# Grouped attention beside a Mish layer, one decode step: a quarter of the last wo's rows loaded early in four 8-row transfers

## The chip, the cores and the metric

The kernel runs on one core of one Trainium2 chip. Times are device microseconds of one execution of the whole program. TensorE is called PE, its weight loads PEld, VectorE DVE, ScalarE ACT, GpSimd POOL and SyncE SP, as the profile does.

## The reference

One decode step for 8 sequences, width 512: the normalised input goes through a grouped-query attention over a cache of 8192 keys (32 query heads, 8 key-value heads of 128) and, beside it, through a dense layer with Mish; both results are added to the input. Everything is float32.

```
xn = layernorm(x)
q  = xn @ wq                          # 8 x 32 heads x 128
o  = softmax(q . k / sqrt(128)) @ v   # each kv head serves 4 query heads, 8192 keys
A  = o @ wo                           # 4096 x 512
h  = xn @ w1 + b1                     # 512 x 1792
B  = (h * tanh(softplus(h))) @ w2     # 1792 x 512
out = x + A + B
```

The key and value caches are 256 MiB each, so the kernel is above all one long load.

## The kernel before

The work is cut into 16 packs: a pack `p` is two of the 8 sequences (`b` = 0, 1) for two of the 8 kv heads, and 4 packs make one head pair `i` (0 to 3). For each `(p, b)` one transfer of 8 MiB brings the keys and one the values, each as 128 partition rows of 64 KiB. `scores` (L348) multiplies the keys with the queries, `rows` (L362), `maximum` (L375), `exponents` (L395), `fold` and `weights` make the softmax weights, `values` (L454) multiplies them with v, `gather` (L468) and `merge` (L484) pick and scale the result. `queries` (L308) makes the queries of a head pair from a block of wq, `outputs` (L530) multiplies a finished head pair with its 2 MiB block of wo.

All big loads go through one list, written out at the start in the order in which they are to be moved (`plan`, L114, and the loops L161 to L181). `pump` (L103) issues them on SP's queue as their places come free. There are three places in SBUF: "a" (64 KiB a partition) for v, "b" (80 KiB a partition) for the keys, which lie in it alternately at its start and 16 KiB further on, and "w" (16 KiB a partition) for wq and wo. A transfer over 128 partitions is cut by partition rows over the 16 DMA engines.

The end of that list is what the change touches. v of the last pack's first sequence goes to "b", v of its second to "a" in two parts (3/4 and 1/4 of the columns). Then follow w2 in four parts (2, 2, 2 and 1 sevenths, W2_PARTS, L177) to "b" and the last block of wo to "w" in two halves of its columns, one half (128 rows of 8 KiB) after the second part of w2 and one after the third.

The end of the computation is written out from L695 on. `values` on the two last v; `down` (L623) multiplies the four parts of w2 as they land; `merge` and `turn` (L507) bring the last head pair's attention output into the layout that wo needs: four matmuls into PSUM, then one copy for each 32 partitions j (L526 on ACT for odd j, L528 on DVE for even j) into `oW`, 128 partitions x 4 x 2 x 8. `last_outputs` (L556) multiplies half of oW's columns with each half of wo and adds to the same PSUM tile `H` as `down`. `keep_busy` (L636) puts a matmul of no use into the gaps. At the end DVE copies `H` (L720) and SP stores it (L721). The instructions of PE, DVE and POOL are held in the order of the program (L725 to L740).

One matmul of float32 shows in the trace as two passes: `down` of a 2/7 part has 16 matmuls and 32 passes.

Of the kernel before, what the change touches and what calls it, by code (L numbers as in the profile page):

```python
# [14 lines left out]
B = 8  # L15
# [8 lines left out]
G = 4  # L24
# [3 lines left out]
BW = 1024  # L28
# [4 lines left out]
Q = P // G  # L33
# [5 lines left out]
PAIRS = HKV // 2  # L39
# [3 lines left out]
HE = P // 2  # L43
# [7 lines left out]
KR = DH * 2 * NB // P  # L51
# [12 lines left out]

QR = CC
OR = 4
W1R = 2 * CC * P // P
W2R = G * FT // 2 * FP // P
FAR = 1e38
# [3 lines left out]
def kernel(  # L73
# [12 lines left out]
    nc = tc.nc  # L86
# [27 lines left out]
    def plan(what, at, blocks, parts=((0, 1),), lo=0):  # L114

        rows = rows_of(blocks)
        n = rows.shape[1]
        t = place[at][:, lo : lo + n]

        def load(cols):  # L120
            nc.sync.dma_start(t[:, cols], rows[:, cols])  # L121
            return t

        for first, end in parts:
            cols = slice(round(first * n), round(end * n))
            queue.append((what, at, lambda cols=cols: load(cols)))


    sc = const.tile([P, 512], F32, name="sc")
# [21 lines left out]
    def plan_v(p, b, at, parts=((0, 1),)):  # L151
        plan(("v", p, b), at, blocks_of(v, p, b), parts)
# [1 line left out]
    def plan_wq(i):  # L154
        plan(("wq", i), "w", wq[i * CC : (i + 1) * CC])

    def plan_wo(i, parts=((0, 1),)):
        plan(("wo", i), "w", wo[i * 4 : i * 4 + 4], parts)


    plan_wq(0)  # L161
# [5 lines left out]
    for p in range(PACKS):  # L167
        for b in range(PB):
            plan_k(p, b)
            if (p, b) in between:  # L170
                what, i = between[p, b]
                (plan_wq if what == "wq" else plan_wo)(i)
            if p > 0:
                plan_v(p - 1, b, "a")
    plan_v(PACKS - 1, 0, "b")
    plan_v(PACKS - 1, 1, "a", ((0, 3 / 4), (3 / 4, 1)))
    W2_PARTS = ((0, 2), (2, 4), (4, 6), (6, 7))  # L177
    for k, (lo, hi) in enumerate(W2_PARTS):
        plan("w2", "b", w2, ((lo / W2R, hi / W2R),))
        if 0 < k < 3:  # L180
            plan_wo(PAIRS - 1, (((k - 1) / 2, k / 2),))  # L181


    S = psum.tile([P, GK], F32, name="s")
# [22 lines left out]
    far = const.tile([P, KINDS], F32, name="far")  # L207
# [12 lines left out]
    aT = const.tile([P, 2 * W2R, Q], F32, name="aT")  # L220
    xw = aT.rearrange("p j q -> p (j q)")[:, : W1R * 2 * B]
    xw = xw.rearrange("p (r t b) -> p r t b", r=W1R, t=2)

    def setup():
# [66 lines left out]
    def setup_w1(wide):  # L291
        for r in range(W1R):
            nc.tensor.transpose(  # L293
                M[:, 64 + r * B : 64 + (r + 1) * B], wide[:, r * P : (r + 1) * P], ident[:B, :B]
            )
        for t in range(2):
            nc.vector.tensor_scalar(
                xw[:, :, t, :],
                M[:, 64 : 64 + W1R * B].rearrange("p (r b) -> p r b", r=W1R),
                half[:, t : t + 1],  # L300
                None,
                op0=ALU.mult,
            )

        nc.gpsimd.memset(pt, 0.0)
# [191 lines left out]

    def turning():

        tid = work.tile([P, HT * KINDS * P], F32, name="e", bufs=1)[:, : OR * P]  # L500
        tid = tid.rearrange("p (r g i) -> p r g i", r=OR, g=G)
        nc.vector.tensor_copy(
            tid, ident.rearrange("p (i r o) -> p r o i", r=OR, o=1).to_broadcast([P, OR, G, Q])
        )
        return tid

    def turn(i, tid):  # L507


        to = oW[i] = work.tile([P, OR, 2, B], F32, name="oW")  # L510
        o = oT.pop(i).rearrange("p n h b -> p (n h b)")
        cols = 2 * REP * B
        for r in range(OR):
            nc.tensor.matmul(
                M[:, 256 + r * cols : 256 + (r + 1) * cols],
                tid[:, r].rearrange("p g i -> p (g i)"),
                o,
                start=True,
                stop=True,
            )  # L520
        m = M[:, 256 : 256 + OR * cols].rearrange("p (r j q) -> p j r q", r=OR, j=G)
        for j in range(G):
            rows = slice(Q * j, Q * (j + 1))
            dst = to[rows].rearrange("p r h b -> p r (h b)")
            if i == PAIRS - 1 and j % 2:
                nc.scalar.copy(dst, m[rows, j])  # L526
            else:
                nc.vector.tensor_copy(dst, m[rows, j])  # L528

    def outputs(i, w):  # L530

# [21 lines left out]
                stop=False,  # L553
            )

    def last_outputs(lo, hi, w):  # L556

        for r in range(lo, hi):
            for h in range(2):
                for g in range(G):  # L560
                    at = r * BW + h * D + g * P
                    nc.tensor.matmul(
                        H[Q * g : Q * g + B, :P],
                        oW[PAIRS - 1][:, r, h, :],
                        w[:, at : at + P],
                        start=False,
                        stop=False,
                    )
# [67 lines left out]
    def keep_busy(n):  # L636

        for k in range(n):
            nc.tensor.matmul(C[0][:Q, :], ones[:, :Q], acc, start=True, stop=True)
# [19 lines left out]
    for p in range(PACKS):  # L659
        for b in range(PB):  # L660
            k = landed.pop(("k", p, b))

            n = PB * p + b - (p > 0)
# [15 lines left out]
            if (p, b) in between:  # L679
                what, i = between[p, b]  # L680
# [14 lines left out]
    p = PACKS - 1  # L695
# [12 lines left out]
    w2_sb, wo_sb = landed["w2"], landed["wo", PAIRS - 1]  # L708
    down(*W2_PARTS[0], w2_sb)
    merge(p, 1)  # L710
    turn(PAIRS - 1, tid)
    down(*W2_PARTS[1], w2_sb)
    last_outputs(0, OR // 2, wo_sb)
    keep_busy(1)
    down(*W2_PARTS[2], w2_sb)
    keep_busy(1)
    last_outputs(OR // 2, OR, wo_sb)
    down(*W2_PARTS[3], w2_sb)
    res = acc[:, :P]
    nc.vector.tensor_copy(res, H[:, :P])  # L720
# [3 lines left out]
    last = {}  # L724
# [54 lines left out]
```

## Time and profile before

| what | value |
|---|---|
| median of 3 runs | 1311.35 us (1311.3 to 1311.6) |
| the profiled execution, its own time | 1311.78 us |
| its span in the profile | 1310.0 us |
| PE busy (share of the span) | 863.7 us (66%) |
| DVE busy | 384.0 us (29%) |
| ACT busy | 111.7 us (9%) |
| POOL busy | 4.8 us (0%) |
| mean granted PE clock | 0.844 |
| HBM read | 561.01 MB, 428 GB/s over the span |
| time of the DMA engines taken by SP's queue q1 | 99.3% |

The span is what the profile's time axis shows, from 0 to 1310.0; some 1.8 us of the execution lie around it. "Share of 16 engines" for a DMA queue is the time of its packets over 16 times the span. In a timeline row stand the start, the time taken, engine, line, operation, the tile written and the tile read, the shape, how many instructions were merged, and in brackets the idle time ahead of them with what ended it. In the chain of waits stand start, time taken and what; a "DMA" piece reaches from the issue of a transfer to its landing. In a table of windows stand the window, its length, PE's busy time, the granted clock, the DMA share and GB/s.

### The profile page before, as it was taken

Reading aid. Unit: us, or ns where it says so; the run is one execution under the profiler, and the core shown is the slowest. Engines: PE = TensorE matmul, PEld = TensorE weight load, DVE = VectorE, ACT = ScalarE, POOL = GpSimd, SP = SyncE. Lnnn points to the kernel's source line nnn. Section 1 sums busy time; section 2 is a strip of 40 time slices with the busy share of each in tenths; the row PEclk is TensorE's granted clock in tenths of the full one; section 3 lists DMA queues with packets and bytes.
Section 4 is the critical chain, followed back from the end, with each engine's and each line's share of the span. In section 5 each row is a group of like instructions: output and inputs, shape, how many; then the busy total and the mean of one; then the engine's idle time right before and its main releaser. Section 6 shows DMA issues by size and latency. Waiting matters only on the chain.

```text
span 1310.0 us, 10715 instructions
## 1 busy us (share of the span) xinstructions
PE 863.7 (66%) x4776; PEld 281.5 (21%) x4776; DVE 384.0 (29%) x590; ACT 111.7 (9%) x294; POOL 4.8 (0%) x10
## 2 busy tenths in 40 slices
PE   4786556866557765677565686655875666766657
PEld 1221112212112221122111222111221221222113
DVE  7150504205051230521405032052320505114051
ACT  1020101001010100101101010010100101001010
POOL 1000000000000000000000000000000000000000
PEclk9887889878799877898878897788877879878789
DMA  9999999999999999999999999999999999999997
GB/s 404 442 423 441 433 429 430 434 437 429 438 431 431 431 439 427 439 423 441 421 444 423 419 447 431 435 427 437 423 425 434 429 439 423 439 431 435 439 425 331
DMA packets 11591, 561.76 MB, mean 429 GB/s; under 512 B 1293, under 2 KB 1425, under 8 KB 1561
## 3 DMA queue, kind: packets, MB, share of 16 engines
q1 hardware_dynamic: 11520, 561.06, 99.3%
q8 instruction: 37, 0.61, 0.2%
q14 instruction: 10, 0.07, 0.0%
q10 hardware_dynamic: 24, 0.02, 0.0%
HBM read 561.01 MB, written 0.07 MB: 428 GB/s over the span
## 4 chain that ended last, share of the span: by engine, by line
DMA 67%; PE 32%; DVE 1%; issue 0%; SPq 0%; ACT 0%; ACTq 0%
DMA kvb<-in_kT 60%; PE c L353 30%; DMA kva<-in_kT 3%; DMA kvb<-in_w 2%; DMA kvb<-in_v 2%; PE o L581 0%; PE h L312 0%; PE o L460 0%; DMA sc<-in_x 0%; SPq L121 0%; DVE nm L379 0%; PE s L365 0%; DVE qT L340 0%; PE m L293 0%; PE o L575 0%
## 5 line engine op out<-in xcount | busy, mean ns | idle before, releaser
L353 PE MATMUL c<-kvb,qT 128*64 128x512 f32 x1984 | 502.4, 671 | 347.3 <-DMA kvb<-in_kT 345.7
L353 PEld LDWEIGHTS c<-kvb,qT 128*64 128x64 f32 x1984 | 162.0, 155 | 687.6 <-issue 470.4
L460 PE MATMUL o<-kva,pt 128*32 128x512 f32 x1984 | 231.4, 620 | 24.2 <-DMA kva<-in_v 24.2
L379 DVE TENSOR_REDUCE nm<-s 128x1 f32<-128x1024 f32 x16 | 19.6, 1225 | 462.2 <-PE s L365 462.2
L412 DVE STREAM_TRANSPOSE raw<-e 128x2048 f32<-128x2048 f32 x32 | 116.0, 3626 | 14.4 <-ACT e L404 12.7
L360 ACT COPY sc<-c 128x512 f32<-128x512 f32 x32 | 18.8, 586 | 1005.0 <-PE c L353 1005.0
L460 PEld LDWEIGHTS o<-kva,pt 128*32 128x32 f32 x1984 | 65.7, 113 | 179.3 <-issue 136.2
L404 ACT ACTIVATE e<-s,nms 128x512 f32<-128x512 f32 x128 | 86.3, 686 | 126.1 <-DVE nms L393 66.8
L492 DVE TENSOR_TENSOR oT<-m,r 128x16 f32<-128x16 f32 x16 | 2.8, 175 | 229.6 <-PE m L488 229.6
L471 DVE TENSOR_SCALAR os<-o,isel 128x128 f32<-128x128 f32 x32 | 11.1, 348 | 155.4 <-PE o L460 155.4
L430 DVE TENSOR_TENSOR pt<-raw 64x256 f32<-64x256 f32 x128 | 53.6, 418 | 2.0
L365 PE MATMUL s<-sc,csel 64*128 64x512 f32 x128 | 36.1, 641 | 8.4 <-ACT sc L360 8.4
L421 DVE TENSOR_TENSOR raw<-raw 128x1024 f32<-128x1024 f32 x32 | 39.2, 1225 | 1.1
L340 DVE TENSOR_TENSOR qT<-qc,bsel 128x1024 f32<-128x1024 f32 x32 | 37.6, 1218 | 0.0
L473 DVE SCALAR_TENSOR_TENSOR os<-o,isel,os 128x128 f32<-128x128 f32 x96 | 33.7, 351 | 3.4
L404 ACT ACTIVATION_READ_ACCUMULATOR e<-s,nms 128x1 f32 x128 | 26.0, 203 | 0.0
L380 PE MATMUL m<-ident,nm 128*1 128x128 f32 x16 | 4.3, 270 | 21.2 <-DVE nm L379 21.2
L312 PE MATMUL h<-kvw,xnT 128*64 128x512 f32 x64 | 16.2, 654 | 0.0
L488 PEld LDWEIGHTS m<-hsel,os 128*128 128x128 f32 x64 | 9.5, 188 | 29.6 <-issue 23.5
L488 PE MATMUL m<-hsel,os 128*128 128x8 f32 x64 | 12.4, 266 | 4.8 <-DVE os L473 3.3
L353 PE MATMUL c<-kva,qT 128*64 128x512 f32 x64 | 14.0, 593 | 1.6 <-DMA kva<-in_kT 1.6
L323 DVE TENSOR_SCALAR e<-h 128x512 f32<-128x512 f32 x16 | 9.9, 684 | 15.9 <-PE h L312 15.9
(100 smaller groups left out, 171.4 us busy)
## 6 DMA issues: line engine op xcount, KB each, us to landing
kvw<-in_wq SPq DMA_DIRECT2D x4, 2048.0 KB, 29.7
kvw<-in_wo SPq DMA_DIRECT2D x3, 2048.0 KB, 30.7
kva<-in_v SPq DMA_DIRECT2D x1, 6144.0 KB, 27.2
kva<-in_w SPq DMA_DIRECT2D x1, 3584.0 KB, 15.8
kvb<-in_w SPq DMA_DIRECT2D x3, 1024.0 KB, 20.6
kva<-in_v SPq DMA_DIRECT2D x1, 2048.0 KB
kvw<-in_wo SPq DMA_DIRECT2D x2, 1024.0 KB, 24.6
kvb<-in_w SPq DMA_DIRECT2D x1, 512.0 KB
```

The lines of the kernel that those rows point to most:

```text
L340: nc.vector.tensor_mul(qT[:, b], qc[:, k * PB + b] .rearrange("p r (o h) -> p r o h", o=1) .to_broadcast([P, KR, KN, REP]), bsel.rearrange ...
L353: nc.tensor.matmul(C[b][HE * c : HE * (c + 1), :], t[:, r], k[:, r * BW + c * 512 : r * BW + (c + 1) * 512], start=(r == order[0]), stop=( ...
L360: nc.scalar.copy(sc, C[b])
L365: nc.tensor.matmul(S[:, c * 512 : (c + 1) * 512], csel[HE * c : HE * (c + 1), b].rearrange("p u b h -> p (u b h)"), sc[HE * c : HE * (c + ...
L379: nc.vector.tensor_reduce(nm, S, axis=AX.X, op=ALU.max, negate=True)
L404: nc.scalar.activation(ex[:, :, s, :], S[:, c * 512 : (c + 1) * 512].rearrange("p (t f) -> p t f", t=HT), AF.Exp, bias=NMS[p][:, s : s + 1 ...
L412: nc.vector.transpose(raw.rearrange("p (m t r) -> p t m r", m=TW, t=HT), ex.rearrange("p t s (q m) -> p t m (s q)", m=TW),)
L421: nc.vector.tensor_add(raw[:, :, :n], raw[:, :, :n], raw[:, :, n:])
L430: nc.vector.tensor_add(pt[rows, b, c].rearrange("p m t e h -> p (m t) e h")[:, :, e], raw[rows, :, at : at + REP], raw[rows, :, V8 + at : ...
L460: nc.tensor.matmul(O[b][Q * c : Q * (c + 1), :], pt[:, b, j % 2, j // 2].rearrange("p t e h -> p (t e h)"), vt[:, W4 * DH * j : W4 * DH * ...
L473: nc.vector.scalar_tensor_tensor(os, O[b][:, DH * i : DH * (i + 1)], isel[:, i : i + 1], os, op0=ALU.mult, op1=ALU.add,)
L488: nc.tensor.matmul(M[:, at : at + 2 * REP], OS.pop((p, b)), hsel, start=True, stop=True)
```

## The change

The last block of wo is 128 rows of 16 KiB. It is no longer loaded as two halves of its columns, but by rows:

- Every fourth row (3, 7, 11, ..., 127) comes ahead of the last v, in four transfers of 8 whole rows. The 16 of them below 64 go to their own partitions of "w" ("near"). The 16 from 64 on go 64 partitions lower, to the same partitions 3, 7, ..., 63, but into the last 16 KiB of "b" ("far"), which the last keys used and the first of the two last v does not.
- The other rows come where the halves came, both after the second part of w2: the even rows in one transfer of 64 rows, then rows 1, 5, 9, ... in one of 32.
- POOL sets the upper 64 partitions of "w" and the lower 64 partitions of the far place to zero ahead of the loads, so that rows which are not there multiply as zero.
- `turn` writes the last head pair's output a second time, partitions 64 to 127 copied to partitions 0 to 63 of the tile `sc` (one copy on DVE, one on ACT).
- `last_outputs` now runs twice over all 4 row groups: once with the far rows and that copy (64 partitions deep), once with the near place, one directly behind the other between the second and the third part of w2. The two filler matmuls there are gone.

```
+QS, QH = 4, 3
...
+    OX_AT = KR * BW
+    last_wo = rows_of(wo[(PAIRS - 1) * 4 :])
+
+    def plan_wo_far():
+
+        n = last_wo.shape[1]
+        near = place["w"][:, :n]
+        far = place["b"][:HE, OX_AT : OX_AT + n]
+
+        def load_near():
+            nc.gpsimd.memset(near[HE:], 0.0)
+            for k in range(QH, 8, QS):
+                nc.sync.dma_start(near[k:HE:8], last_wo[k:HE:8])
+            return near
+
+        def load_far():
+            nc.gpsimd.memset(far, 0.0)
+            for k in range(QH, 8, QS):
+                nc.sync.dma_start(far[k:HE:8], last_wo[HE + k :: 8])
+            return far
+
+        queue.append((("wo", PAIRS - 1), "w", load_near))
+        queue.append(("wo far", "behind b", load_far))
+
+    def plan_wo_rest(first, step):
+        n = last_wo.shape[1]
+        t = place["w"][:, :n]
+
+        def load():
+            nc.sync.dma_start(t[first::step], last_wo[first::step])
+            return t
+
+        queue.append((("wo", PAIRS - 1), "w", load))
...
     plan_v(PACKS - 1, 0, "b")
+    plan_wo_far()
     plan_v(PACKS - 1, 1, "a", ((0, 3 / 4), (3 / 4, 1)))
     W2_PARTS = ((0, 2), (2, 4), (4, 6), (6, 7))
     for k, (lo, hi) in enumerate(W2_PARTS):
         plan("w2", "b", w2, ((lo / W2R, hi / W2R),))
-        if 0 < k < 3:
-            plan_wo(PAIRS - 1, (((k - 1) / 2, k / 2),))
+        if k == 1:
+            plan_wo_rest(0, 2)
+            plan_wo_rest(1, 4)
...
+        if last:
+
+            oX = oW["far"]
+            for j in range(G // 2, G):
+                rows = slice(Q * j, Q * (j + 1))
+                dst = oX[Q * j - HE : Q * (j + 1) - HE].rearrange("p r h b -> p r (h b)")
+                if j % 2:
+                    nc.scalar.copy(dst, m[rows, j])
+                else:
+                    nc.vector.tensor_copy(dst, m[rows, j])
...
-    def last_outputs(lo, hi, w):
-
-        for r in range(lo, hi):
+    def last_outputs(o, w):
+
+        for r in range(OR):
             for h in range(2):
                 for g in range(G):
                     at = r * BW + h * D + g * P
                     nc.tensor.matmul(
                         H[Q * g : Q * g + B, :P],
-                        oW[PAIRS - 1][:, r, h, :],
+                        o[:, r, h, :],
...
     merge(p, 1)
+
+    oW["far"] = sc[:HE, : OR * 2 * B].rearrange("p (r h b) -> p r h b", r=OR, h=2)
     turn(PAIRS - 1, tid)
     down(*W2_PARTS[1], w2_sb)
-    last_outputs(0, OR // 2, wo_sb)
-    keep_busy(1)
+    last_outputs(oW["far"], landed["wo far"])
+    last_outputs(oW[PAIRS - 1], wo_sb)
     down(*W2_PARTS[2], w2_sb)
-    keep_busy(1)
-    last_outputs(OR // 2, OR, wo_sb)
     down(*W2_PARTS[3], w2_sb)
```

More of the change, by code (lines that the diff above doesn't have):

```diff
@@ L155, in plan_wq, with plan_wo @@
         plan(("wq", i), "w", wq[i * CC : (i + 1) * CC])
-    def plan_wo(i, parts=((0, 1),)):
-        plan(("wo", i), "w", wo[i * 4 : i * 4 + 4], parts)
+    def plan_wo(i):
+        plan(("wo", i), "w", wo[i * 4 : i * 4 + 4])
+    OX_AT = KR * BW
[23 more added lines that the diff above has]
+        queue.append((("wo", PAIRS - 1), "w", load))
     plan_wq(0)
@@ L507, in turn @@
     def turn(i, tid):
+        last = i == PAIRS - 1
         to = oW[i] = work.tile([P, OR, 2, B], F32, name="oW")
@@ L524, in turn @@
             dst = to[rows].rearrange("p r h b -> p r (h b)")
-            if i == PAIRS - 1 and j % 2:
+            if last and j % 2:
                 nc.scalar.copy(dst, m[rows, j])
```

## The prediction

> **What bounds the kernel now.** I read the page's transfer rows first, then the chain of waits, then the end of the span with the DMA view cut into narrow windows.
>
> ```profile
> span 1310.0 us, 10715 instructions
> ...
> DMA  9999999999999999999999999999999999999997
> ...
> DMA packets 11591, 561.76 MB, mean 429 GB/s; under 512 B 1293, under 2 KB 1425, under 8 KB 1561
> ...
> q1 hardware_dynamic: 11520, 561.06, 99.3%
> q8 instruction: 37, 0.61, 0.2%
> ...
> q10 hardware_dynamic: 24, 0.02, 0.0%
> ```
>
> The 16 DMA engines are busy in every slice but the last, and one queue, q1 (SP's), fills 99.3% of their time. A kernel like this ends when the slowest of 16 engines has moved its share. At 429 GB/s an engine moves 26.8 GB/s, so a 16 KiB row costs one engine 16384 / 26.8e3 = **0.61 us**. That is the unit of this forecast.
>
> The chain of waits at its end, in order of time (start, us, what):
>
> ```profile
> 1247.64 25.68 DMA kvb<-in_v
> ...
> 1278.57 1.21 SPq L121
> ...
> 1279.82 26.57 DMA kvb<-in_w
> 1306.39 0.04 issue
> 1306.43 0.67 PE h L628 x16
> ```
>
> The last transfer, the last seventh of w2, lands at 1306.39. Behind it stand only 16 matmul passes, then a copy and the store. An earlier last landing moves the end by as much, until PE is late instead.
>
> Now the stagger of the engines. Three windows over the time in which the first three quarters of the last v land, the first data that the tail works on; then the drain from 1300 to 1306.4 in 40 slices of 0.16 us. Each engine ends its part of a transfer with one packet under 512 B, so that count says how many engines are done.
>
> ```profile
> DMA packets 38, 0.75 MB, mean 343 GB/s; under 512 B 8, under 2 KB 8, under 8 KB 8
> ...
> DMA packets 35, 0.59 MB, mean 421 GB/s; under 512 B 5, under 2 KB 5, under 8 KB 5
> ...
> DMA  9596969898897969564636366503122322100000
> GB/s 666 205 563 256 563 282 512 358 461 358 358 410 307 384 256 384 230 282 179 256 154 256 154 256 205 230 26 128 77 102 102 128 102 102 77 26 26 0 0 0
> ...
> q1 hardware_dynamic: 286, 1.49, 56.4%
> ...
> 1287.91 4.69 PEld L460 LDWEIGHTS o<-kva,pt 128*32 128x32 f32 x48 [0.46 <-DMA kva<-in_v]
> ```
>
> Between 1283.0 and 1285.2 **eight** engines finish, between 1285.2 and 1286.6 five more, and the last three only by 1287.9, where PE, released by that transfer, loads its first weights for it. So eight engines run early, at least 2.7 us ahead of the last. No later transfer mends it, since each gives every engine an equal share. The drain shows the same: from the 28th slice (1304.3) never more than 128 GB/s, five engines' worth. The rest of the work is 56.4% of 6.4 us = 3.61 us of all 16 engines: shared out evenly it would end near 1303.6. **No rebalancing of this tail can win more than 2.8 us.**
>
> Why eight? The page counts 37 instruction fetches on q8, 16 KiB each. Following each data packet to the one that begins where it ends (the packet records, which no view prints), I find the fetches falling in turn on eight engines only, and these are the late ones. This sets chances below, no term.
>
> **The change part by part.** *The short transfers.* An 8-row transfer uses eight engines, one row each: q10 holds the x load (8 rows) and the b1 load (4 rows) and shows 24 packets, 12 rows and 12 completions; a transfer over all 16 would add 16 completions. After the change eight engines get 4 early rows, and the two remaining transfers give each of 16 engines 4 + 2 rows. Before, each engine had the equivalent of 8. So the eight carry 10 rows (+2, **+1.22 us**), the others 6 (−2, **−1.22 us**). I take the eight to be the early ones.
>
> [...] The four engines that I followed from the b1 load all seem to be of the early kind, one with a doubt.
>
> *Late engines.* Last landing 1306.39 − 1.22 = 1305.17; the third part of w2 (1 MiB, 64 KiB on each engine, 2.44 us; the last part, 32 KiB, 1.22 us) lands at 1303.95, the rest of wo at 1301.51. *Early engines.* At least 2.7 us ahead, so done by 1303.7, with 1.22 more by 1304.9: still not last. On the way they are 4 rows (2.44 us) later on the last v and on w2's first half, less than their 2.7 us lead, so PE's starts there stay. Gain on the landing: **1.22 us**.
>
> *SP's queue and POOL.* Two of the short transfers stand behind a memset of 64x4096, and the last v behind them on SP.
>
> ```profile
> 1234.44 16.59 PE L353 MATMUL c<-kvb,qT 128*64 128x512 f32 x64 [10.60 <-DMA kvb<-in_kT]
> ...
> 1247.64 0.33 SPq L121 DMA_DIRECT2D kvb<-in_v  x1
> 1260.69 0.33 SPq L121 DMA_DIRECT2D kva<-in_v  x1
> ...
> 11.09 2.12 DVE L286 COPY csel<-ident 64x64 f32<-64x64 f32 x4
> 11.29 1.84 POOL L305 MEMSET pt<- 128x2048 f32 x1 [1.20 <-PE m L293]
> ...
> 1254.85 0.21 DVE L386 COPY nx<-nr 1x128 f32<-1x128 f32 x1
> ```
>
> The memset may start when the last score matmul has read that place, 1234.44 + 16.59 = 1251.03. The nearest row is 2048 elements in 1.84 us: 4096 should take 3.7 (an estimate; at least 1.84), so it ends about 1254.7. Two issues follow at 0.33 (this row) to 1.21 us each (1278.57 above): SP is free by 1257.1. Before, SP issues the last v only at 1260.69, waiting for PE. Cover 3.6 us: cost **nothing**; it would cost only with a memset over 7 us, and even then up to 1268 or so the queue still holds the transfer issued at 1247.64. The other memset waits for wo's third block, long used. The rest of wo and w2's last two parts wait on SP for the four short transfers; these end behind the last v but one on the early engines, about when that lands as a whole (1247.64 + 25.68 = 1273.3), and SP issues that part of the tail only around 1278.57: nothing again. A memset can hold up DVE: at 11.29 the four small copies beside it took 2.12 us instead of some 0.2 each. The copy nx at 1254.85 comes just behind; if the memset ran 0.5 us longer, so would what follows, and 0.3 of it is covered (below). Value 0, bounds 0 and +0.5.
>
> *PE and the copies.* The timeline of the tail:
>
> ```profile
> 1298.57 1.06 PE L628 MATMUL h<-kvb,aT 128*8 128x128 f32 x32
> 1298.68 0.21 DVE L528 COPY oW<-m 32x64 f32<-32x64 f32 x1 [1.20 <-PE m L514]
> 1298.92 0.20 ACT L526 COPY oW<-m 32x64 f32<-32x64 f32 x1 [33.75 <-DVE oW L528]
> ...
> 1299.42 0.20 ACT L526 COPY oW<-m 32x64 f32<-32x64 f32 x1 [0.29 <-DVE oW L528]
> ...
> 1300.33 1.06 PE L562 MATMUL h<-kvw,oW 128*8 128x128 f32 x32 [0.70 <-DMA kvw<-in_wo]
> 1301.20 1.02 PE L639 MATMUL c<-acc,ones 128*32 128x512 f32 x2
> ...
> 1305.18 1.06 PE L562 MATMUL h<-kvw,oW 128*8 128x128 f32 x32 [0.56 <-DMA kvw<-in_wo]
> 1306.43 0.62 PE L628 MATMUL h<-kvb,aT 128*8 128x128 f32 x16 [0.19 <-DMA kvb<-in_w]
> ```
>
> The copies alternate between DVE and ACT, each waiting for the other, about 0.25 apart; two more end at 1299.42 + 0.20 + 2 x 0.25 = 1300.12. 32 passes take 1.06, 16 take 0.62: 0.0275 a pass plus 0.18 at the end. Added are 64 passes for the far rows (1.76 us); removed are the two filler matmuls of 1.02. Then: far 1300.17 to 1301.93; near (rest of wo landed 1301.51) to 1303.69; third part of w2 at its landing, 1303.99 to 1304.9; last part at 1305.21, ending 1305.21 + 0.62 = 1305.83. Before, 1306.43 + 0.62 = 1307.05. PE waits 0.3 us for each of the last two landings: that is the cover of the added 1.76 us, of the two copies and of a late DVE. Without it, each microsecond there is paid in full.
>
> *The clock without the fillers.* Two pairs of PE windows (us, PE busy, granted clock, DMA):
>
> ```profile
> 1212.50:1215.90 3.40, 0.99 (x10) 1.00 1.16 501
> 1215.90:1219.30 3.40, 3.40 (x20) 0.50 0.93 405
> 1301.25:1304.65 3.40, 2.87 (x44) 1.00 0.63 255
> 1304.65:1308.05 3.40, 1.68 (x48) 1.00 0.08 31
> ```
>
> With 0.99 us of work in 3.4 the clock was halved right after; with 1.68 it still stood at 1.00. In the new tail any such window holds about 1.8 us or more, so I take no loss; half a clock on the last 16 passes and part of those before would be +0.3 to +0.9.
>
> **Sum:** −1.22 + 0. The profiled execution took 1311.78 (1310.0 and 1.8 around it) and should be 1310.56; the median shown is 0.43 lower, 1311.35, so **1310.1 us**. The change is −0.09%, below what a measurement of this kernel tells from no change (0.2%, 2.6 us).
>
> **Rivals.** *The short rows collide (slower side).* All 32 early rows go into partitions 3, 7, 11 ... 59, so two of the eight engines may write into one place at a time. If pairs in step share one engine's rate, 4 rows cost 4.88 us instead of 2.44, and the early engines end up to 2.44 later: 1304.9 + 2.44 = 1307.3 instead of 1306.39, so 1311.35 + 0.95 = **1312.3**. It decides from 0.3 us extra on, where the early become last, and turns into a loss from 1.5. The same bound holds if PE starts late on the last v: its chain then ends with that landing. Against it: at 429 GB/s in all, engines are at full rate in each stage, and pairs out of step by a row would not meet. Chance 0.14, any price between 1310.4 and 1312.3.
>
> [...]
>
> *The eight are the late ones.* Then these carry +1.22: 1311.35 + 1.22 = **1312.6**. The followed packets speak against it: 0.05. *PE becomes the bound* through the copies, the 64 passes, DVE behind the memset or the halved clock: **1310.4 to 1311.0**, 0.07. *Nothing is shifted*, the rows being spread over 16 engines: **1311.3**, 0.02. *A stall of SP or a broken order of landings* over 2.6 us: 0.03. *More than forecast*, at most 2.8 us by the drain: 1308.5, 0.01.
>
> **How the numbers follow.** The forecast, 1310.1, has the remaining 0.68, with its own range 1309.7 to 1310.5. The range 1309.6 to 1311.7 takes in that, PE as bound, the unshifted case and about half of the collisions, 0.84 in all; left out are late eight, hard collisions and the stall. Only the stall and part of its neighbours lie over 2.6 us slower: 0.04. Over 2.6 us faster: 0.01. Within: 0.95.
>
> **What would show it.** Right: the window of the drain holds fuller slices up to 1304.9 and is empty after 1305.2; last landing of in_w near 1305.2; PE's far passes start near 1300.2 with ACT as the releaser; a POOL memset of 64x4096 of about 3.7 us near 1251; SP's last v still near 1260.7; PEclk 1.00 in the tail. Wrong: PE starting on the last v after 1287.9 (collision, or the late eight); eight engines still moving after 1306; L628 waiting for PE rather than for in_w; nx later than 1255; a halved clock after 1301.

## The result, and the profile after

| | before | after |
|---|---|---|
| median | 1311.45 us (1311.30 to 1311.63, 6 runs) | 1316.35 us (1314.69 to 1317.51, 6 runs) |
| profiled execution, its span | 1311.78, 1310.0 | 1314.69, 1312.9 |

The ratio is 1.0037, with a 95% interval of 1.0024 to 1.005: the change makes the kernel slower by about 4.9 us. The forecast was 1310.1, with a range that ended at 1311.7. The profiled execution of after is the fastest of its six, so its trace shows 2.9 us of the loss.

The rows of the page of after that answer to those of before. The work is the same, and so is the share of the one queue. The rate (GB/s) stands lower in one of the 40 slices, the last but one (some 1247 to 1280 us): 383 in place of 425. The last has 330 and had 331. First before's row of rates, then the rows of after.

```profile
GB/s 404 442 423 441 433 429 430 434 437 429 438 431 431 431 439 427 439 423 441 421 444 423 419 447 431 435 427 437 423 425 434 429 439 423 439 431 435 439 425 331
```

```profile
span 1312.9 us, 10849 instructions
...
DMA  9999999999999999999999999999999999999997
GB/s 403 443 432 430 440 428 424 440 430 436 431 436 436 428 432 438 422 444 424 436 431 424 432 436 430 440 424 438 422 436 435 428 434 438 422 446 418 440 383 330
...
q1 hardware_dynamic: 11424, 561.06, 99.3%
```

The DMA engines are as busy in that slice as in the others (9) and move less. Busy is not fast: a packet that takes longer counts as busy for longer. To find the place, three windows of each kernel, first before, then after. The columns are the length of the window, the busy times of PE, PEld, DVE, ACT and POOL with their instructions, the granted PE clock, the DMA share and GB/s.

```profile
1256.00:1266.00 10.00, 6.73 (x62) 1.99 (x54) 7.10 (x9) 5.47 (x16) 0.00 (x0) 1.00 0.99 427
1268.00:1276.00 8.00, 2.54 (x13) 0.69 (x17) 6.29 (x10) 0.00 (x0) 0.00 (x0) 0.50 0.97 418
1278.00:1288.00 10.00, 8.53 (x67) 2.86 (x63) 1.57 (x5) 0.00 (x0) 0.00 (x0) 1.00 0.97 414
```

```profile
1256.00:1266.00 10.00, 6.64 (x54) 1.81 (x46) 8.27 (x11) 3.69 (x12) 0.00 (x0) 0.94 1.05 448
1268.00:1276.00 8.00, 0.40 (x4) 0.23 (x8) 5.09 (x10) 0.00 (x0) 0.00 (x0) 0.50 1.03 285
1278.00:1288.00 10.00, 8.53 (x69) 2.90 (x62) 1.57 (x5) 0.00 (x0) 0.00 (x0) 0.84 0.96 415
```

In the 8 us from 1268 the rate falls from 418 to **285 GB/s** at a DMA share of 1.03, and it stands at 415 again from 1278 on (414 before). That is when the short rows move (1267.6 to 1276.2 in the packet records, which no view prints): they are queued behind the transfer that before's chain shows landing at 1273.3. In those 8 us (418 − 285) x 8 = 1.06 MB stay unmoved, 2.5 us of all 16 engines at 429 GB/s. Half the rate on the eight engines with short rows alone would leave three quarters, some 314 of 418; 285 is lower. That **the other engines are slowed too** is in the packet records as well: the 16 KiB rows took 0.65 to 1.3 us (half of them 0.98 or more) in place of 0.61, and the 64 KiB packets of ordinary rows that begin in this window 3.6 to 4.4 in place of 2.42. Followed from packet to packet, each of the eight engines without short rows has long ones: seven of them 64 KiB packets, the longest of each 3.48 to 3.91 us, the eighth 48 KiB packets of 2.83 and 2.85 in place of 1.82.

What this does further on, first two rows of before, then the timeline of after (`o` is what the last two v are multiplied into; L639 and L689 are the filler matmuls ahead of the last v):

```profile
1273.46 8.97 PE L460 MATMUL o<-kvb,pt 128*32 128x512 f32 x64 [7.98 <-DMA kvb<-in_v]
...
1284.77 3.60 PE L639 MATMUL c<-acc,ones 128*32 128x512 f32 x8
```

```profile
1249.32 3.50 POOL L179 MEMSET kvb<- 64x4096 f32 x1 [149.78 <-PE c L392]
...
1252.85 1.17 SPq L181 DMA_DIRECT2D kvb<-in_wo  x2
1253.07 0.22 DVE L425 COPY nx<-nr 1x128 f32<-1x128 f32 x1
...
1260.60 0.34 SPq L124 DMA_DIRECT2D kva<-in_v  x1
...
1275.61 9.82 PE L499 MATMUL o<-kvb,pt 128*32 128x512 f32 x64 [11.33 <-DMA kvb<-in_v]
...
1287.76 4.86 PE L689 MATMUL c<-acc,ones 128*32 128x512 f32 x7
...
1292.04 0.63 PE L499 MATMUL o<-kva,pt 128*32 128x512 f32 x3
...
1304.60 0.21 ACT L576 COPY sc<-m 32x64 f32<-32x64 f32 x1 [0.28 <-DVE sc L578]
...
1304.90 1.93 PE L612 MATMUL h<-kvb,sc 64*8 64x128 f32 x64 [0.58 <-issue]
1306.76 1.93 PE L612 MATMUL h<-kvw,oW 128*8 128x128 f32 x64
...
1308.51 1.49 PE L678 MATMUL h<-kvb,aT 128*8 128x128 f32 x48
1310.07 0.29 DVE L770 COPY acc<-h 128x128 f32<-128x128 f32 x1 [5.51 <-PE h L678]
```

PE starts on the last v at 1292.04; in the kernel before, it did so at 1287.92. Two things are late there, each by about as much. One is that transfer's landing (KB, us from issue to landing, first before, then after): issued at 1260.7 and 1260.6, it lands at 1287.9 and 1291.7.

```profile
kva<-in_v SPq DMA_DIRECT2D x1, 6144.0 KB, 27.2
```

```profile
kva<-in_v SPq DMA_DIRECT2D x1, 6144.0 KB, 31.1
```

The other is PE itself. The v ahead of it lands at 1275.5 in place of 1273.3, after PE has been idle for 11.33 us in place of 7.98, and from 1276 to 1292 PE was granted a lower clock (first two windows before, then two after; the clock stands ahead of the DMA share):

```profile
1276.00:1284.00 8.00, 6.76 (x58) 2.10 (x50) 1.40 (x5) 0.00 (x0) 0.00 (x0) 0.92 1.01 432
1284.00:1292.00 8.00, 7.78 (x57) 3.55 (x61) 0.17 (x2) 0.00 (x0) 0.00 (x0) 1.00 0.93 393
```

```profile
1276.00:1284.00 8.00, 8.00 (x56) 2.20 (x52) 0.00 (x0) 0.00 (x0) 0.00 (x0) 0.68 0.96 412
1284.00:1292.00 8.00, 6.53 (x34) 1.94 (x27) 1.57 (x5) 0.00 (x0) 0.00 (x0) 0.79 0.95 407
```

The multiplication with that v took 9.82 us in place of 8.97, and the fillers were still running when the last v had landed; before, PE's weight loads sat idle for 0.46 us until that landing. From 1292 on PE's chain runs without a wait for a transfer: the far pass at 1304.90, the near pass at 1306.76, the last two parts of w2 in one run of 48 passes, to 1310.00. Before, the last pass ended at 1307.05: 2.95 us earlier, which is the difference of the spans (2.9). The drain, in the same window as in the prediction, shows that the transfers are late by themselves: where before's slices stood at 0 by 1306.4, the last five here are still at 2 to 6 tenths.

```profile
DMA  9299949793959696989949797979696958352665
...
q1 hardware_dynamic: 320, 2.25, 84.1%
```

### The profile page after: what moved, and what is told of

Its sections match the earlier page's. It is cut to its first block, busy times and chain, and to the rows that moved or that the text cites. A ratio compares the mean times of both kernels' runs of the same rounds, so it can differ in the third digit from the quotient of the medians.

```text
span 1312.9 us, 10849 instructions
## 1 busy us (share of the span) xinstructions
PE 864.9 (66%) x4836; PEld 281.6 (21%) x4836; DVE 385.0 (29%) x591; ACT 111.9 (9%) x295; POOL 11.9 (1%) x12
## 4 chain that ended last, share of the span: by engine, by line
DMA 60%; PE 35%; DVE 4%; issue 1%; ACT 0%; SPq 0%; ACTq 0%; DVEq 0%
DMA kvb<-in_kT 54%; PE c L392 31%; PE o L499 3%; DMA kva<-in_kT 3%; DMA kvb<-in_v 2%; DMA kva<-in_w 1%; DVE raw L451 1%; DVE pt L469 1%; PE o L631 0%; DVE os L512 0%; PE c L689 0%; DVE nm L418 0%; DVE raw L460 0%; PE s L404 0%; PE h L612 0%
## 5 line engine op out<-in xcount | busy, mean ns | idle before, releaser
L392 PE MATMUL c<-kvb,qT 128*64 128x512 f32 x1984 | 495.7, 663 | 350.4 <-DMA kvb<-in_kT 316.7
L499 PE MATMUL o<-kva,pt 128*32 128x512 f32 x1984 | 236.7, 630 | 22.8 <-DMA kva<-in_v 22.8
L499 PE MATMUL o<-kvb,pt 128*32 128x512 f32 x64 | 9.8, 782 | 11.3 <-DMA kvb<-in_v 11.3
```

The costliest lines, as they stand in the source:

```text
L392: nc.tensor.matmul(C[b][HE * c : HE * (c + 1), :], t[:, r], k[:, r * BW + c * 512 : r * BW + (c + 1) * 512], start=(r == order[0]), stop=( ...
L499: nc.tensor.matmul(O[b][Q * c : Q * (c + 1), :], pt[:, b, j % 2, j // 2].rearrange("p t e h -> p (t e h)"), vt[:, W4 * DH * j : W4 * DH * ...
```

## The experiments

Theories at the start. **P**: rows that different engines write into neighbouring partitions collide in SBUF (the prediction's rival). **S**: source rows 128 KiB apart collide where they are read. **E**: a transfer over eight engines alone slows everything. A fourth, **H**, was formed from the runs. Each edit is against the changed kernel unless said; a kernel that ran once has one time and no interval. "The window" is 1268 to 1276 us; the last number of its row, the rate, says whether the dip is there.

**e1_step4.** The same rows, but each 8-row transfer takes every fourth partition in place of every eighth.

```diff
-            for k in range(QH, 8, QS):
-                nc.sync.dma_start(near[k:HE:8], last_wo[k:HE:8])
+            for k in (QH, QH + 32):
+                nc.sync.dma_start(near[k : k + 29 : 4], last_wo[k : k + 29 : 4])
...
-            for k in range(QH, 8, QS):
-                nc.sync.dma_start(far[k:HE:8], last_wo[HE + k :: 8])
+            for k in (QH, QH + 32):
+                nc.sync.dma_start(far[k : k + 29 : 4], last_wo[HE + k : HE + k + 29 : 4])
```

> Same rows early, but each 8-row transfer takes every fourth row of one quarter (3 to 31, 35 to 63, 67 to 95, 99 to 127), written to partitions 4 apart; source rows 64 KiB apart instead of 128. In the changed kernel the DMA engines together fall from 418 GB/s (kernel before) to 285 in the window 1268 to 1276. Theory P (the 8 rows written 8 partitions apart collide in SBUF): back over 400 GB/s in that stretch, time 1310.1 to 1312.6 (the upper end if two of the eight engines are late ones). Theory S (8 source rows 128 KiB apart collide in HBM): at least partly better, 1311 to 1315. Theory E (a transfer over eight engines alone slows all): unchanged, about 285 GB/s and 1315 to 1317.

Measured: 1312.55 (1311.16 to 1314.36, 10 runs) against 1311.51, ratio 1.0008, interval 0.9999 to 1.0018. The window of e1:

```profile
1268.00:1276.00 8.00, 3.01 (x16) 0.89 (x20) 5.95 (x10) 0.00 (x0) 0.00 (x0) 0.52 0.98 424
```

The dip is gone (285 to 424 GB/s), and with it 3.8 of the 4.9 us. E falls: these transfers too have 8 rows, and those of after went over eight engines (packet records, as above). About 1 us of loss is left between the medians, though the interval just takes in none; e7 and e14 look into it.

**e2_src_contig** and **e3_dst_step4.** One alters the source only, the other the destination only. So e2 loads other rows of wo than the computation's, and e3 puts the right ones into wrong partitions; the amounts are the same. First e2's edit, then e3's.

```diff
-                nc.sync.dma_start(near[k:HE:8], last_wo[k:HE:8])
+                nc.sync.dma_start(near[k:HE:8], last_wo[2 * (k - QH) : 2 * (k - QH) + 8])
```

```diff
-                nc.sync.dma_start(near[k:HE:8], last_wo[k:HE:8])
+                nc.sync.dma_start(near[QH + 8 * (k - QH) : QH + 8 * (k - QH) + 29 : 4], last_wo[k:HE:8])
```

The far rows are altered in the same way.

> Written as in the changed kernel, 8 partitions apart, but each transfer reads 8 neighbouring rows of wo (16 KiB apart), so the wrong rows of wo are multiplied. Theory P: about 285 GB/s in the stretch of the short rows, 1314.7 to 1317.5. Theory S: over 400 GB/s, 1310 to 1312.6. Theory E: about 285 GB/s.

> Read as in the changed kernel (source rows 128 KiB apart), but written to partitions 4 apart (3 to 31, 35 to 63), so rows of wo meet the wrong rows of the attention output. Theory P: over 400 GB/s in the stretch, 1310 to 1312.6. Theory S: about 285 GB/s, 1314.7 to 1317.5. Theory E: about 285 GB/s.

Measured: e2 1314.9, e3 1312.1 (one run each). The window of e2, then of e3:

```profile
1268.00:1276.00 8.00, 0.26 (x4) 0.23 (x8) 6.42 (x10) 0.00 (x0) 0.00 (x0) 0.50 1.03 279
```

```profile
1268.00:1276.00 8.00, 2.84 (x16) 0.91 (x20) 5.62 (x10) 0.00 (x0) 0.00 (x0) 0.50 1.03 442
```

The destination decides, the source doesn't: S falls.

**e4_rows16.** Two transfers of 16 rows, by the expectation over all 16 engines, every fourth partition of the lower half.

```diff
+            for k in (QH,):
+                nc.sync.dma_start(near[k:HE:4], last_wo[k:HE:4])
...
+            for k in (QH,):
+                nc.sync.dma_start(far[k:HE:4], last_wo[HE + k :: 4])
```

> The same 32 rows come early, but as two transfers of 16 rows over all 16 engines, one row each, partitions 4 apart; no engine gets more than another. Theory E: over 400 GB/s and the time of the kernel before, 1311.0 to 1311.6. Theory P: two engines a place, as in the changed kernel, so below 400 GB/s for some 5 us, 1312.5 to 1315. Theory S: over 400 GB/s, 1311.0 to 1312.

Measured: 1315.45 (1314.36 to 1317.33, 9 runs), ratio 1.003, interval 1.002 to 1.004; 291 GB/s in the window. The partitions are those of e1; only the cut into transfers differs, and with it, as the expectation takes it, the engines that write them. The dip is back (291 GB/s in place of 424), so it is not the partitions alone; what is left is which engine writes which.

**e5_direct.** As e1, but the upper rows go to their own partitions (67 to 127); no far place, no memset, no second pass.

```diff
+            for k in (QH, QH + 32, QH + 64, QH + 96):
+                nc.sync.dma_start(near[k : k + 29 : 4], last_wo[k : k + 29 : 4])
```

> As the variant with steps of 4, but the rows of the upper half go to their own partitions (67 to 95, 99 to 127), so there is no far place, no memset, no second copy of the output and no second pass of 64. If engines of the upper half write there at their full rate already, theory P (places collide) says that these two transfers slow the machine again: about 300 GB/s for half as long as in the changed kernel (some 4 us), 1312 to 1314. If P holds only between the short rows themselves: over 400 GB/s throughout and, PE having 1.76 us less to do, 1310.0 to 1311.5.

Measured: 1314.94 (1313.22 to 1316.57, 10 runs), ratio 1.0025, interval 1.0015 to 1.0034; 301 GB/s in the window. The detour of the upper rows by the lower half, with its 64 passes, is worth more than it costs: written straight into the upper half, they dip.

**e7_no_far_pass.** As e1, without the 64 passes on the far rows, so that these are missing from the sum. It asks whether e1's last 1 us is PE's.

```diff
-    last_outputs(oW["far"], landed["wo far"])
```

> The variant with steps of 4 without the 64 passes over the far rows, so these rows' part of the result is left out; loads as there. If what is left of its loss (median 1312.55, 1311.16 to 1314.36) is PE becoming the bound: 1310.1 to 1311.3 and a spread under 1.5 us. If it is two late engines among the eight: unchanged, 1312 to 1313 with the same spread.

Measured: 1312.61 (1310.46 to 1313.29, 10 runs), ratio 1.0005, interval 0.9995 to 1.0014. With 1.9 us of PE work less it is no faster than e1, so the rest isn't that pass's. Its profiled execution (1312.76) ends behind the last transfer, which lands at 1307.4, 1.0 us later than before's (1306.39):

```profile
1279.47 27.95 DMA kvb<-in_w
```

**e6_adjacent** and **e8_half.** e6 puts each transfer's 8 rows into 8 neighbouring partitions (again wrong ones for the computation); e8 is e1 for the far rows and the changed kernel for the near ones.

```diff
+                nc.sync.dma_start(near[4 * (k - QH) : 4 * (k - QH) + 8], last_wo[k:HE:8])
...
+                nc.sync.dma_start(far[4 * (k - QH) : 4 * (k - QH) + 8], last_wo[HE + k :: 8])
```

```diff
+            for k in (QH, QH + 32):
+                nc.sync.dma_start(far[k : k + 29 : 4], last_wo[HE + k : HE + k + 29 : 4])
```

> As the changed kernel, but each 8-row transfer writes 8 adjacent partitions (0 to 7 or 16 to 23), so rows of wo meet wrong rows of the output. If a place is 4 neighbouring partitions, four rows meet in each of two places: theory P says worse than the changed kernel, under 250 GB/s while they move and 1317 to 1322. If only a distance of 8 collides: over 400 GB/s, 1311 to 1313.

> Near rows as in the changed kernel (8 apart), far rows 4 apart. Theory P: half the dose, the low rate (about 285 GB/s) for some 4 us instead of 8.5, time 1312.5 to 1315. If any collision sets the whole loss: 1314.7 to 1317.5.

Measured (one run each): e6 1317.57 and 242 GB/s in the window; e8 1315.33 and 293. The window of e6:

```profile
1268.00:1276.00 8.00, 0.00 (x0) 0.00 (x0) 6.28 (x10) 0.00 (x0) 0.00 (x0) 0.50 1.05 242
```

Neighbouring partitions gave the lowest rate of these runs, 242 GB/s. Half the dose dips as deep in this window, and by the packet records below it costs less in all (37 engine-us in place of 53).

**e9_ladder.** A try to tell the eight engines apart: transfers of 1, 2, ... 8 rows, 36 in all, in their own partitions; no far place and no second pass. All 36 are loaded again with the rest, in two transfers of 64 rows.

```diff
+            for n, k in enumerate((0, 1, 2, 3, 32, 33, 34, 35)):
+                nc.sync.dma_start(near[k : k + 4 * n + 1 : 4], last_wo[k : k + 4 * n + 1 : 4])
```

> To tell the engines apart: ahead of the last v eight transfers of 1, 2, ... 8 rows, partitions 4 apart in the lower half, so that the first engine gets eight extra rows, the next seven, and so on (all 36 are loaded again with the rest; one pass of 64 at the end, no far place, no memset). With 36 rows (0.59 MB) more in all the time says little: 1312 to 1316. Rate while the short rows move: over 400 GB/s, as no two of one transfer share a place. If two of the first eight engines are late ones: two of the eight ladders belong to engines that are hit by instruction fetches. If none: no ladder is hit.

Measured: 1317.75 (one run), for a reason of its own. SP's issues in e9:

```profile
1246.35 0.33 SPq L124 DMA_DIRECT2D kvb<-in_v  x1
1246.73 26.69 SPq L173 DMA_DIRECT2D kvw<-in_wo  x8
1273.53 0.85 SPq L124 DMA_DIRECT2D kva<-in_v  x2
```

Eight transfers behind the 8 MiB one keep SP for 26.69 us; the last v is issued at 1273.53 (1260.60 in after), and the engines run dry (8 GB/s from 1272 to 1274). Two and two (1.39 and 1.17 us of SP in after) cost nothing. What SP waited for between the eight (us in total, times, longest):

```profile
SPq L173 <- DMA kvb<-in_v: 18.6, 1, 18.6
...
SPq L173 <- DMA kva<-in_v: 2.6, 1, 2.6
```

So the hold is above all a wait for the 8 MiB transfer's landing. In the trace's records the transfers share eight landing semaphores in turn: the eighth short one takes that of the 8 MiB one and is issued when that has landed, at 1272.7. The question that the ladder was for stayed unanswered; that each of its transfers begins with the same engine, as the expectation takes it, no run shows.

**e10_rows16_low.** Only 16 early rows, 1, 5 ... 29 and 3, 7 ... 31, at their own partitions; the rest as transfers of 64 and 48 rows.

```diff
+            for k in (1, 3):
+                nc.sync.dma_start(near[k : k + 29 : 4], last_wo[k : k + 29 : 4])
...
-            plan_wo_rest(1, 4)
+            plan_wo_rest(33, 2)
```

> 16 early rows instead of 32 (1, 5, ... 29 and 3, 7, ... 31, 4 apart, in their own partitions), the other 112 rows in two transfers over all 16 engines; no far place, no memset, no second pass, PE has the passes of the kernel before. Half the shift: +0.61 us on the eight, -0.61 on the others. If two late engines among the eight set the end: 1311.8 to 1312.3, half the loss of the variant with 32 rows 4 apart (+1.0). If the eight were all early ones: 1310.6 to 1311.0.

Measured: 1318.28 (1317.52 to 1319.75, 4 runs), ratio 1.0054, interval 1.0037 to 1.007: a miss. Three windows of e10:

```profile
1268.00:1276.00 8.00, 2.64 (x16) 0.78 (x20) 6.15 (x10) 0.00 (x0) 0.00 (x0) 0.50 0.99 426
...
1292.00:1300.00 8.00, 6.45 (x82) 2.94 (x70) 1.99 (x7) 0.20 (x1) 0.00 (x0) 1.00 1.07 353
1300.00:1308.00 8.00, 1.28 (x36) 0.92 (x40) 0.03 (x1) 0.21 (x1) 0.00 (x0) 0.56 0.86 214
```

The early rows run clean, and the dip sits in the tail, where the 48-row transfer (33, 35 ... 127: three rows for each engine, if they are shared out evenly) moves. The chain of waits ends behind its landing, at 1307.8:

```profile
1278.01 29.76 DMA kvw<-in_wo
```

Which engine writes which of its rows no record says.

**e11_home.** Two transfers of 16 rows, 3, 11 ... 123 and 7, 15 ... 127, at their own partitions, to control for whole rows that come early. The edit is against e5. I took engine j's ordinary rows to be the eight partitions 8j to 8j+7.

```diff
-            for k in (QH, QH + 32, QH + 64, QH + 96):
-                nc.sync.dma_start(near[k : k + 29 : 4], last_wo[k : k + 29 : 4])
+            for k in (QH, QH + 4):
+                nc.sync.dma_start(near[k::8], last_wo[k::8])
```

> The 32 early rows go by two transfers of 16 rows (3, 11, 19 ... 123 and 7, 15 ... 127), one row on each of the 16 engines, each row into a partition that its engine also writes in the ordinary transfers; no far place, no second pass, no memset. P (rows written by engines of two kinds into one place at a time): no collision, 425 GB/s or more from 1268 to 1276 us, and since no engine carries more than another nothing is shifted: 1311.2 to 1311.8, within 0.05% of the kernel before, and PE starts on the last v near 1288. If it is enough for a collision that whole 16 KiB rows come early (any partition): 270 to 310 GB/s in that window and 1314 to 1316. If e1's loss of 1.0 us comes from the order of the transfers and not from two late engines among the eight: 1312.3 to 1312.8 with a clean window.

Measured: 1315.45 (1314.75 to 1316.49, 7 runs), ratio 1.0028, interval 1.0017 to 1.004; the window of e11:

```profile
1268.00:1276.00 8.00, 0.47 (x4) 0.23 (x8) 5.72 (x10) 0.00 (x0) 0.00 (x0) 0.50 1.00 272
```

P in this form falls. What fits all the runs is **H**, a supposition: no record names the engine that moved a packet or the partition that it went to, so H is judged by the rates alone, its engine numbers stand for the order of the rows, and what makes two writers slow each other in one place no run shows. H supposes that each engine has a home, the partitions that it writes in the ordinary transfers, that row j of an 8- or 16-row transfer goes to engine j, and that a row which an engine writes in another's home meets the ordinary rows that the owner is writing there. The homes are fitted to the rates from 1268 to 1276 us:

- Row j of an 8-row transfer runs clean at partitions 3+4j and 35+4j (e1, 424 GB/s) and at 1+4j (e10, 426), and not at a step of eight (after, 285) or of one (e6, 242). So engine j (0 to 7) gets 1+4j to 3+4j and the same 32 higher. 4j and 32+4j are counted with them, though no run speaks for it: of the early rows only some of e6 and e9 lie there.
- The upper half is not home to these eight (e5, 301), and 16 rows that all go to the lower half dip (e4, 291). So engine 8+j gets the same 64 higher; no run tells one of these eight from another.

In e1, each row is at home. In the changed kernel row j goes to 3+8j or 7+8j: one of eight at home.

**e12_shift.** The test of H against P: as e1, but the near rows land four partitions higher (7, 11 ... 35 and 39, 43 ... 67) and the far ones in 6, 10 ... 34 and 7, 11 ... 35, so that it sums other rows than the computation's; the edit is against e1. No two rows of a transfer share a home, but none is at its own.

```diff
-                nc.sync.dma_start(near[k : k + 29 : 4], last_wo[k : k + 29 : 4])
+                nc.sync.dma_start(near[k + 4 : k + 33 : 4], last_wo[k : k + 29 : 4])
...
-            for k in (QH, QH + 32):
+            for k in (6, 7):
```

> As e1 (8-row transfers, step 4), but the rows go four partitions (far: three or four) higher: 7, 11 ... 35 and 39, 43 ... 67, far 6, 10 ... 34 and 7, 11 ... 35. Wrong rows, and the far pass reads them, so that the output is not the reference's; bytes, engines and passes are those of e1. Within one such transfer no two rows lie in the same group of four partitions or 32 apart, just as in e1; but row number j of each lies where, by the runs so far, engine j+1 writes its ordinary rows, and in e1 where engine j itself does. P (two of the short rows in one place at a time): no collision, 425 GB/s or more from 1268 to 1276 us and 1312.0 to 1312.9. H (each engine has a place of its own, two groups of four partitions 32 apart, and a row written into another engine's place collides with that engine's ordinary rows): 250 to 310 GB/s there and 1314 to 1317. H is what e11 calls for: its 16 rows, row j to partition 3+8j, lie at home for engines 0 and 8 alone.

(What it says of e11 holds, by H, for the first of its two transfers; in the second, engines 7 and 15 are at home.) Measured: 1317.54 (1316.67 to 1320.05, 5 runs), ratio 1.0048, interval 1.0034 to 1.0062; two windows of e12:

```profile
1268.00:1276.00 8.00, 0.00 (x0) 0.00 (x0) 6.92 (x10) 0.00 (x0) 0.00 (x0) 0.50 1.03 285
1276.00:1284.00 8.00, 7.04 (x56) 2.18 (x60) 0.00 (x0) 0.00 (x0) 0.00 (x0) 0.76 0.94 350
```

**H holds and P falls**: four partitions of shift cost 5.0 us (1312.55 to 1317.54), though no two rows of one short transfer share a home.

**e13_home32** and **e14_extra16.** e13 loads the 32 early rows by one transfer over all 128 partitions, two rows for each engine, if they are shared out evenly, and needs no far place. e14 loads 16 rows a second time by two transfers of 8 rows, at home by H, which nothing reads. e13's edit is against e11, e14's against e13.

```diff
-            for k in (QH, QH + 4):
-                nc.sync.dma_start(near[k::8], last_wo[k::8])
+            for k in (QH,):
+                nc.sync.dma_start(near[k::4], last_wo[k::4])
```

```diff
+            for k in (QH, QH + 32):
+                nc.sync.dma_start(far[k : k + 29 : 4], last_wo[k : k + 29 : 4])
```

> The 32 early rows by one transfer (rows 3, 7 ... 127 to partitions 3, 7 ... 127), two rows on each of 16 engines; no far place, no second pass, no memset. H (each engine has a place of its own: two groups of four partitions, 32 apart) with the ordinary rows shared out by that place: each engine gets the two rows of its own place, so no collision, 425 GB/s or more from 1268 to 1276 us, and as no engine carries more than another the time of before: 1311.1 to 1311.8. If rows that come early collide wherever their transfer reaches over all 128 partitions (as e5, e11 could also be read): 270 to 310 GB/s and 1314 to 1316.

> e13 and two transfers of 8 rows more (step 4, to partitions 3 ... 31 and 35 ... 63 of the far place), which load 16 rows a second time and which nothing reads: two rows more on each of the eight engines that carry them, 1.22 us each, none on the others; each row at home by H, so a clean window. If two late engines are among the eight (the reading of e1 and e7): 1.0 to 1.3 us over e13. If all eight are early, as the prediction took it: 0 to 0.3 over e13. If the rows were spread over all 16 engines: 0.6.

Measured: e13 1311.51 (1311.17 to 1313.16, 11 runs) against 1311.57, ratio 0.9998, interval 0.9989 to 1.0007; e14 1312.25 (1311.40 to 1314.14, 11 runs), ratio 1.0005, interval 0.9996 to 1.0014. The window of e13, then of e14:

```profile
1268.00:1276.00 8.00, 2.83 (x16) 0.91 (x20) 6.05 (x10) 0.00 (x0) 0.00 (x0) 0.50 0.95 412
```

```profile
1268.00:1276.00 8.00, 3.23 (x16) 0.90 (x20) 5.44 (x10) 0.00 (x0) 0.00 (x0) 0.50 1.02 440
```

Early rows over all 128 partitions can run clean and take the time of before. That each lies at home supposes that this transfer, too, is shared out by home; with that, it settles what e5 and e11 left open. The medians of e13 and e14 are 0.74 us apart, between the 0 to 0.3 for early engines and the 1.0 to 1.3 for late ones, nearest to the 0.6 for rows spread over 16 engines, and the runs overlap. Spread they were not: from 1262 to 1279.5 the page counts 48 packets under 512 B, 16 for v, 16 for the 32-row transfer and 8 for each short one. So e14 doesn't settle whether late engines are among the eight.

The runs with 32 early rows, by how many of the 32 are not at home ("abroad") under H:

| kernel | not at home | GB/s, 1268 to 1276 | us |
|---|---|---|---|
| e1, e3, e7, e13 | 0 | 424, 442, 401, 412 | 1312.55, 1312.1, 1312.61, 1311.51 |
| e8 | 14 | 293 | 1315.33 |
| e4, e5 | 16 | 291, 301 | 1315.45, 1314.94 |
| after, e2, e6, e11 | 28 | 285, 279, 242, 272 | 1316.35, 1314.9, 1317.57, 1315.45 |
| e12 | 32 | 285, then 350 | 1317.54 |

e10's 16 early rows and all 48 of e14 are, by H, at home too: 426 and 440.

The excess over the usual time of a packet, added up over all 16 engines from the packet records, is about 1 engine-us with no row abroad, 37 with 14, 44 and 48 with 16, 53 to 66 with 28 and 63 with 32: **some 2 to 3 engine-us for each row abroad**, where a row alone takes 0.61.

## Why the prediction was wrong

*What bounds the kernel* was right for before. For after it holds no longer: after's end is PE's chain behind the late v, itself slowed by a lower clock (0.68 and 0.79 from 1276 to 1292), and the transfers are late beside it.

*The short transfers*, one row each on eight engines: right in count. The +1.22 and −1.22 take the same eight for all four transfers, which no run shows ahead of the change; in the packet records of after, followed from packet to packet, eight engines carry four 16 KiB rows each and eight carry none. Their price, 0.61 us a row, is **the step that failed**. It was taken from a mean rate at which every engine writes at home, and, by H, a row abroad isn't that operation: in after 28 rows cost 53 engine-us beyond what the packets usually take. Spread over 16 engines that is 3.3 us, in place of the +1.22 and −1.22 of the sum, and the last v landed 3.8 us later.

*The rival of colliding short rows* had, by H, the right kind of mechanism and the wrong partner. It let pairs of short rows meet and argued that "pairs out of step by a row would not meet". By H the partner is the owner of the place, which writes there nearly all the time, in step or not; and the price falls on all engines, not on the pair. So its 1312.3 was too low. That short rows meet among themselves was an assumption that no run ahead of it shows, and it doesn't explain e12, where no two of a transfer share a home and the window shows 285 GB/s.

*"I take the eight to be the early ones"*: not settled. Following packets past the instruction fetches, I find six of the eight early and two late (in after these two begin on their short rows at 1272.4, the six between 1267.6 and 1269.9); e1 and e7, without a dip, end 1.0 us above before, near the rival's 1312.6 for late eight, and e7's last landing is late by as much. So even with the placement mended the forecast of −1.22 does not come. e1's profiled execution (1311.16) is its fastest, and its range reaches up to 1314.36, so this part rests on medians.

*"On the way they are 4 rows later ... so PE's starts there stay"*: wrong through the same step. PE starts on the last v 4.1 us later, and its own chain up to there is late as well, through the late landing of the v ahead and a lower clock.

*SP and POOL*: right. The memset took 3.50 us (3.7 estimated), SP issued the last v at 1260.60 (1260.69 before), and nx took its 0.22 at 1253.07: no hold-up.

*PE and the copies*: the size was right, 1.93 us for 64 passes (1.76 and 0.18) and the last copy 0.50 after the fourth's end (1304.31 to 1304.81; 0.5 estimated). Both stood behind the late v. In e1, where PE starts on the last v at 1288.66 (1287.92 before), the far pass starts at 1300.70 (forecast 1300.17) and PE waits 0.15 us for each of the last two landings, as the timeline of e1 shows; the cover of 0.3 was half used.

```profile
1288.66 7.07 PE L499 MATMUL o<-kva,pt 128*32 128x512 f32 x64 [1.36 <-DMA kva<-in_v]
...
1300.70 1.93 PE L612 MATMUL h<-kvb,sc 64*8 64x128 f32 x64 [0.58 <-issue]
...
1304.65 1.06 PE L678 MATMUL h<-kvb,aT 128*8 128x128 f32 x32 [0.15 <-DMA kvb<-in_w]
1305.86 0.62 PE L678 MATMUL h<-kvb,aT 128*8 128x128 f32 x16 [0.15 <-DMA kvb<-in_w]
```

*The clock* stood at 1.00 from 1292 to 1308 in after: no loss there, as forecast. The forecast looked only at the tail without its fillers; what was lost came ahead of it, 0.68 and 0.79 in place of 0.92 and 1.00 from 1276 to 1292, behind PE's longer wait.

No version that I ran beats the kernel before; e13 takes its time (1311.51 against 1311.57).

## What to carry to other kernels

When a transfer over part of the partitions runs beside full ones, ask which engine writes which partition, not only how many bytes each engine carries: by H, row j of a short transfer belongs where engine j writes its ordinary rows (here a step of four partitions from the lower half's first four, 424 GB/s in e1, or one transfer over all 128 partitions at a step of four, 412 in e13). A dip shows as a low GB/s at a full DMA share (285 at 1.03 here); the busy strip hides it. A late transfer can cost twice: PE, idle for 11.33 us in place of 7.98, went on here at a clock of 0.68 in place of 0.92. Taking load from the engines that end last is worth nothing until one knows which engines these are.

## What the runs showed that I had not expected

- Rows written in another engine's home, as H has it, slow all 16 engines: 285 GB/s in place of 418 for 8 us, with 64 KiB packets of up to 3.9 us in place of 2.42 on engines that carry no short row. By what path no run shows.
- Eight short transfers queued behind an 8 MiB one held SP for 26.69 us, until that one had landed (e9); two took 1.39.
- A 48-row transfer at a step of two ran at 214 to 353 GB/s in its windows (e10), where the 64- and 32-row ones of e1 left 426 from 1292 to 1300.
